# Attention and ELU on one core: first q and k turned half by half, conversion steps spread over the first group's units

## The chip, the cores and the metric

The kernel runs on one core of one Trainium2 chip. The metric is the device time of one execution in microseconds (us), lower is better. Names of engines: PE is TensorE, DVE is VectorE, ACT is ScalarE, POOL is GpSimd, SP is SyncE, which issues most of the DMAs here. PEld is PE's weight load.

## The reference

Routed attention first, then a two-layer product with an ELU between:

```python
batch, n_heads, seq, head_dim = (4, 8, 768, 64); n_clusters = 16
q_assign = np.argmax(np.einsum('bhsd,hcd->bhsc', q_n, c_n), axis=-1)   # q_n, k_n, c_n: unit rows
k_assign = np.argmax(np.einsum('bhsd,hcd->bhsc', k_n, c_n), axis=-1)
mask = q_assign[:, :, :, None] == k_assign[:, :, None, :]
scores = np.where(mask, 0.125 * np.matmul(q, k.transpose(0, 1, 3, 2)), -1e9)
attn_out = np.matmul(softmax(scores), v)
x = attn_out.transpose(0, 2, 1, 3).reshape(3072, 512)
h = x @ w_in                                        # 512 x 2048
g = np.where(h > 0.0, h, np.exp(np.minimum(h, 0.0)) - 1.0)
return (g @ w_out).astype(np.float32)               # 2048 x 512
```

The two weights come as 8-byte floats. The kernel reads them as pairs of 32-bit words and puts float32 weights together itself.

## The kernel before

**Slots.** Attention goes through 32 blocks n = (batch b, half of the queries, pair of heads pr); eight blocks make a batch. `slot(n)` computes the scores of block n, while the value product of block n-1 and the division of block n-2 run beside it. On PE a slot is: `row_sums` (L550) of n-2, `values` (L532) of n-1, sometimes `clusters_q` or `clusters_k` (L423), then six times a `plain` product (L494) and a `masked` one (L507) into one of three two-bank tiles of a ring. ACT turns each into exponentials (L516). DVE adds them (`sums_begin` L519, `sums_end` L524 and L525), divides (`divide` L564, L565; its last product L568 is on POOL), and transposes the next batch's k and q blocks (L634, L641, L645). "Slot n begins" below means where PE's first L532 of that slot stands in the trace.

**Clusters.** For each half, L423 compares q or k with the centroids; the told chain on DVE (L436, L438, L439, L449) finds the best cluster and transposes the marks; two ACT copies (L452) bring them to the other half of the partitions; for q, `mask_q` (L459, two operations on POOL) makes the mask that `masked` needs. The ACT copies and what follows wait in a list `later` until `flush()` is called.

**Start.** q and k of the first batch are loaded row by row and turned on PE: `turned_by_pe` (L573) is a product with the identity. One two-bank tile takes two pairs of q (one bank each, copied out by L584 on ACT and L586 on DVE), or both halves of one pair of k (L596). After all of k is turned, both halves' clusters are computed; the first three `plain` products stand ahead of telling them. q's second half and the batches after come in blocks that DVE transposes: `load_q` issues 16 DMAs, `load_k` 4, `load_v` 1, all on SP, all in the order of the program.

**Conversion.** Both weights come in 16 pieces of 1 MB (8 of w_in, 8 of w_out). `ask` (L296) loads a piece's words into a free place (`places`: words_w, parts of w_out's own space, and `spare`, each good up to some piece). A piece then takes four steps: `begin` (L316 and L324 on DVE, with an activation L326 on ACT put in `later`), and three times `join` (L336, L340, L346 on DVE); the second join frees the place, which may ask for the next piece. Four `weight_sum` steps (L371 to L377, DVE) follow. `weigh(n)` hands out steps by credit: each slot adds ROOM[n] to at most 2.5 that is left, and a begin costs 1.4, a join 1.25, a sum 2.2; no join follows a begin in the same slot, and a begin waits until its piece was asked for two slots earlier.

**First group's units.** The rows of x go in six groups of 512. The first product of a group takes four units of seven block products (L726), by a scheme of partial sums: PE writes one bank, ACT copies it into the next as the start of another sum (L766, L778), other copies go aside (L770, L786), DVE adds them in (L779, L788). `elu_exp` is an exponential on ACT (L736) and a clip on POOL (L737); `elu` (L740) and a difference (L805) are on DVE. The last part of a unit is put in `behind` and runs after the first product of the next one. `w_step` (L705, L707, L709 on POOL, each with a DMA L710) prepares the next unit's weights, `x_sum_step` (L682 to L688) the sums of x. `unit` calls `fill()` at four places. In the first group it does nothing before the change; there `weigh(32 + u)` hands out steps after each unit. The second product (L910) of the group comes next.

Of the kernel before, what the change touches and what calls it, by code (L numbers as in the profile page):

```python
# [61 lines left out]
def main_path(ctx, tc, c, q, k, v, centroids, moe_w_in, moe_w_out, out):  # L62
# [121 lines left out]
    def rows_of(t, src):  # L184
# [14 lines left out]
    first_k = [  # L199
        rows_of(t, k[0, 2 * pr : 2 * pr + 2]) for pr, t in enumerate(raw_k + kT[1][2:])  # L200
    ]
    load_v(0)
    load_q(0, 1)

# [62 lines left out]
    ]  # L267
    words, asked_in, now = {}, {}, -2
    asked, split, joined = 0, 0, 0
# [97 lines left out]
    def weight_sum(n):  # L367
# [12 lines left out]
    ROOM = (  # L380
        [2.3, 2.6, 3.0, 3.0, 1.4, 1.7, 2.6, 2.6] * (B - 1)
        + [2.3, 2.6, 4.0, 4.0, 3.0, 3.0, 3.0, 3.0]
        + [4.0, 5.0, 5.0, 5.0]
    )
# [12 lines left out]
    def weigh(n):  # L397
        nonlocal credit, now
        now = n
        credit = min(credit, 2.5) + ROOM[n]  # L400
        begun = False
        while steps and credit >= COST[steps[0][0]]:
            kind, m = steps[0]
            if kind == "join" and begun or kind == "sum" and n < len(blocks) + 2:
                return
            if kind == "begin" and asked_in.get(m, n) > n - 2 and n < len(blocks):
                return
            credit -= COST[kind]
            begun = begun or kind == "begin"
            weigh_step(*steps.pop(0))  # L410
# [165 lines left out]

    for two in range(2):
        ps = ring()
        for e in range(2):
            pr = 2 * two + e  # L580
            for t in range(HT):
                turned_by_pe(ps[:, e, ts(t, P)], first_q[pr], t)
            if e == 0:
                nc.scalar.copy(qT[0][pr], ps[:, e, :HS])  # L584
            else:
                nc.vector.tensor_copy(qT[0][pr], ps[:, e, :HS])  # L586
    nc.tensor.transpose(o_bank[:, :P], work[:, : 2 * D], ident)
    nc.vector.tensor_copy(cT, o_bank[:, :P])
    clusters_q(0, 0, d_bank)()
    flush()  # L590
    for pr in range(NPR):
        ps = ring()
        for t in range(NT):
            turned_by_pe(ps[:, t // HT, ts(t % HT, P)], first_k[pr], t)
        copy = nc.vector.tensor_copy if pr % 2 else nc.scalar.copy
        copy(kT[0][pr].rearrange("p (h s) -> p h s", h=2), ps[:, :, :HS])  # L596
    told = [clusters_k(0, half, ps) for half, ps in ((0, o_bank), (1, d_bank))]
    begun = [ring() for _ in range(3)]
    for kt in range(3):
        plain(0, kt, begun[kt])  # L600
    told[0]()
    flush()
    told[1]()
    ask()


    def slot(n):
# [41 lines left out]
        if n == 0:  # L649
            for kt in range(NT):  # L650
                s = begun[kt] if kt < 3 else ring()
                if kt >= 3:
                    plain(n, kt, s)
                masked(n, kt, s)
                exponential(kt, s)
                if kt == 2:
                    flush()
                elif kt == 3:
                    sums_begin()
            flush()  # L660
            return
        for kt in range(NT):
# [15 lines left out]
    def x_sum_step(k_, n):  # L678
        x11, x12, x21, x22 = x_parts(k_)
        t1, t2, t4 = x_s  # L680
        if n == 0:
            nc.gpsimd.tensor_tensor(t1, x12, x11, op=Alu.subtract)  # L682
        elif n == 1:
            nc.gpsimd.tensor_tensor(t2, x22, t1, op=Alu.subtract)
        elif n == 2:
            nc.gpsimd.tensor_tensor(x12, x22, x12, op=Alu.subtract)
        else:
            nc.gpsimd.tensor_tensor(t4, x21, t2, op=Alu.subtract)  # L688

# [430 lines left out]
    last_n = len(blocks) - 1  # L1120
    for n in range(len(blocks)):
        slot(n)
# [12 lines left out]
    values(last_n)  # L1135
    sums_end()
    take_sums(last_n - 1)
    divide(last_n - 1)
# [308 lines left out]
```

## Time and profile before

| what | us |
|---|---|
| median of three runs (lowest, highest) | 922.06 (921.91, 922.33) |
| the profiled execution | 922.52 |
| its span, first to last instruction | 920.7 |
| start, to the first L532 | 28.49 |
| slots 1 to 31 | 312.30 |
| last value product and the first group's units, to the first L910 | 60.33 |
| the rest | 519.58 |

The span leaves out about 1.8 us around the instructions. A profile row says: start and length in us, engine, line, operation, what it writes and reads, shapes, how many instructions were merged, and in brackets the idle time of its engine before it with what ended that wait. One float32 product of the program is two MATMUL rows. "SPq" is SP issuing a DMA. Groups read: busy time, mean ns of one, then idle time before them and its causes. A row by stretch ends with the granted clock of PE, the busy share of the DMA engines and GB/s.

### The profile page before, as it was taken

How to read it: one execution, taken by the hardware profiler on the slowest of the kernel's cores; microseconds unless marked ns; L12 is line 12 of the kernel's file. 1: busy time of each engine (PE TensorE's matmuls, PEld its weight loads, DVE VectorE, ACT ScalarE, POOL GpSimd, SP SyncE). 2: the span in 40 equal slices, each digit the busy share in tenths (PEclk: the TensorE clock that was granted, in tenths of full speed). 3: DMA queues.
4: the chain of work that ended last, by engine and by line, in shares of the span. 5: the costliest groups of instructions: out<-in, count | busy, mean ns of one | idle time of the engine just before them, and what ended most of it. 6: DMA issues, size and time to landing. Idle time of an engine off the chain costs nothing.

```text
span 920.7 us, 15833 instructions
## 1 busy us (share of the span) xinstructions
PE 900.6 (98%) x6080; PEld 686.5 (75%) x6083; DVE 672.9 (73%) x980; ACT 412.1 (45%) x811; POOL 207.4 (23%) x201
## 2 busy tenths in 40 slices
PE   7999999999999998999999999999999999999996
PEld 5444444444444447899988998999899989998996
DVE  4899999999999995772289953595359535953574
ACT  2777687777777773320133223322332233223321
POOL 1112020231303463850024102310231023102200
PEclk9999999999999999999999999999999999999999
DMA  6774564354425221110198762176217621762172
GB/s 166 220 189 88 135 155 87 127 101 90 115 82 141 94 86 69 68 47 1 58 288 307 257 198 60 46 255 195 66 46 255 198 64 45 252 203 64 44 224 81
DMA packets 143331, 121.22 MB, mean 132 GB/s; under 512 B 88208, under 2 KB 104592, under 8 KB 142224
## 3 DMA queue, kind: packets, MB, share of 16 engines
q1 hardware_dynamic: 142000, 115.93, 42.9%
q0 software_dynamic: 1248, 4.20, 1.5%
q8 instruction: 50, 0.82, 0.4%
q14 instruction: 33, 0.27, 0.1%
HBM read 100.96 MB, written 18.09 MB: 129 GB/s over the span
## 4 chain that ended last, share of the span: by engine, by line
PE 77%; DVE 15%; issue 3%; POOL 2%; ACT 1%; SPq 1%; DMA 1%; DVEq 0%; POOLq 0%; ACTq 0%
PE bank L910 22%; PE bank L726 21%; PE o_bank L532 8%; PE banks L494 8%; PE o_bank L910 4%; PE o_bank L726 4%; PE d_bank L910 2%; DVE sums_w L524 2%; DVE sums_w L519 2%; PE banks L507 2%; PE d_bank L726 2%; PE d_bank L550 2%; DVE sums_w L525 1%; POOL kq_g L737 1%; PE banks L573 1%
## 5 line engine op out<-in xcount | busy, mean ns | idle before, releaser
L516 ACT ACTIVATE p_out<-banks 128x768 f32<-128x768 f32 x192 | 154.3, 811 | 25.2 <-PE banks L507 21.2
L737 POOL TENSOR_SCALAR kq_g<-kq_g 128x512 f32<-128x512 f32 x96 | 71.4, 753 | 397.9 <-ACT kq_g L736 397.5
L532 PE MATMUL o_bank<-p_out,kq_g 128*64 128x384 f32 x768 | 129.3, 486 | 0.0
L532 PEld LDWEIGHTS o_bank<-p_out,kq_g 128*64 128x64 f32 x768 | 55.1, 137 | 68.8 <-issue 63.4
L740 DVE SCALAR_TENSOR_TENSOR kq_g<-kq_g,bank 128x512 f32<-128x512 f32 x72 | 48.2, 683 | 72.2 <-POOL kq_g L737 72.2
L726 PE MATMUL bank<-xT,w_in 128*128 128x256 f32 x384 | 90.7, 379 | 0.1
L568 POOL TENSOR_TENSOR xT<-xT,sums_w 128x384 f32<-128x384 f32 x32 | 35.9, 1120 | 203.4 <-DVE sums_w L565 176.1
L726 PEld LDWEIGHTS bank<-xT,w_in 128*128 128x128 f32 x384 | 72.6, 190 | 10.1
L726 PE MATMUL bank<-xT,spare 128*128 128x256 f32 x288 | 67.7, 386 | 3.6 <-ACT bank L778 3.6
L726 PE MATMUL bank<-x_sum,w_in 128*128 128x256 f32 x288 | 68.0, 379 | 0.0
L726 PEld LDWEIGHTS bank<-xT,spare 128*128 128x128 f32 x288 | 55.7, 194 | 11.7 <-POOL kq_g L737 4.0
L524 DVE TENSOR_TENSOR sums_w<-sums_w,p_out 128x1536 f32<-128x1536 f32 x32 | 61.4, 1918 | 3.3
L910 PE MATMUL bank<-w_out,kq_g 128*128 128x128 f32 x512 | 62.9, 275 | 0.0
L910 PEld LDWEIGHTS bank<-w_out,kq_g 128*128 128x128 f32 x512 | 60.4, 192 | 0.3
L519 DVE TENSOR_TENSOR sums_w<-p_out 128x1536 f32<-128x1536 f32 x32 | 58.9, 1842 | 2.0 <-ACT p_out L516 2.0
L726 PEld LDWEIGHTS bank<-x_sum,w_in 128*128 128x128 f32 x288 | 54.6, 190 | 7.3
L736 ACT ACTIVATE kq_g<-bank 128x512 f32<-128x512 f32 x72 | 41.9, 598 | 39.3 <-PE bank L726 39.1
L970 DVE TENSOR_TENSOR kq_g<-kq_g 128x1024 f32<-128x1024 f32 x36 | 43.7, 1221 | 5.3 <-PE bank L910 5.3
L459 POOL TENSOR_SCALAR kq_g<-w_out,big,minus 128x768 bf16<-128x768 bf16 x16 | 32.7, 2052 | 59.1 <-ACT w_out L452 59.1
L494 PE MATMUL banks<-kq_g 64*128 64x384 f32 x192 | 39.7, 492 | 0.7 <-ACT p_out L516 0.7
L494 PE MATMUL banks<-x_sum,xT 64*128 64x384 f32 x192 | 39.6, 493 | 0.6 <-ACT p_out L516 0.6
L494 PE MATMUL banks<-kq_g,xT 64*128 64x384 f32 x192 | 39.6, 491 | 0.0
(233 smaller groups left out, 1707.5 us busy)
## 6 DMA issues: line engine op xcount, KB each, us to landing
spare<-w_far SPq DMA_DIRECT2D x60, 256.0 KB, 2.7
kq_g<-in_v_dram SPq DMA_DIRECT2D x32, 384.0 KB, 3.6
sums_w<-far_s_s SPq DMA_DIRECT2D x40, 256.0 KB, 4.0
words_w<-far_s_s SPq DMA_DIRECT2D x29, 256.0 KB, 3.4
words_w<-in_moe_w_out_dram SPq DMA_DIRECT2D x6, 1024.0 KB, 5.0
out_dram<-p_out SPq DMA_DIRECT2D x24, 256.0 KB, 2.6
w_out<-in_q_dram SPq DMA_DIRECT2D x112, 48.0 KB, 2.4
words_w<-far_a_s SPq DMA_DIRECT2D x21, 256.0 KB, 3.5
```

Of the source, the lines that this page charges most:

```text
L494: nc.tensor.matmul(s[:, e, :HS], lhsT=kT[b % 2][pr][rows, ts(kt, P)], rhs=qT[half][pr][rows], start=True, stop=False,)
L516: nc.scalar.activation(probs[kt], s[:, :, :HS], Act.Exp, scale=SCALE)
L519: nc.vector.tensor_tensor(add_to, probs_all[:, : 4 * HS], probs_all[:, 4 * HS : 8 * HS], op=Alu.add)
L524: nc.vector.tensor_tensor(add_to, add_to, probs_all[:, 8 * HS :], op=Alu.add)
L532: nc.tensor.matmul(o_bank[64 * e : 64 * e + 64, :HS], lhsT=v_raw[n % 2][:, e, kt], rhs=probs[kt][:, e], start=(kt == 0), stop=(kt == NT - 1),)
L568: nc.gpsimd.tensor_tensor(x_of(n), x_of(n), r_of, op=Alu.mult)
L726: nc.tensor.matmul(bank[:, ts(f, QS)], lhsT=left[:, ch, ts(f, P)], rhs=right[:, ch], start=first and f == 0 and ch == 0, stop=ch == 1, ski ...
L736: nc.scalar.activation(to, bank.rearrange("p (f n) -> p f n", f=2), Act.Exp)
L737: nc.gpsimd.tensor_scalar(to, to, 1.0, 0.0, op0=Alu.min, op1=Alu.max)
L740: nc.vector.scalar_tensor_tensor(to, to, -1.0, bank.rearrange("p (f n) -> p f n", f=2), op0=Alu.add, op1=Alu.max)
L910: nc.tensor.matmul(bank[:, :P], lhsT=left[:, f], rhs=right[:, f], start=first and f == 0, stop=last and f == 3, skip_group_check=True,)
L970: nc.vector.tensor_tensor(b[to][:, f], b[x][:, f], b[y][:, f], op=op)
```

## The change

First loads: the third and fourth pair of k now go where q's second half is to come, v of block 1 is loaded at once, and q's second half later. q and k are turned one half of one pair at a time, each into one bank, six banks in turn, and copied by ACT alone; clusters of k's first half are told while the second half is turned. Block 0's scores follow in a part of their own, `slot_first`, with no conversion step. q's second half is transposed in slot 2 and told in slot 3. ROOM is smaller in the first batch and at the end of the last. The last place for words, p_out, is added after the last value product. All steps that are left run one by one in the four `fill` places of the first group's units. The first group's sums of x go from POOL to DVE.

```diff
     first_k = [
-        rows_of(t, k[0, 2 * pr : 2 * pr + 2]) for pr, t in enumerate(raw_k + kT[1][2:])
+        rows_of(t, k[0, 2 * pr : 2 * pr + 2])
+        for pr, t in enumerate(raw_k + [raw_q_all[:, :S], raw_q_all[:, S:]])
     ]
     load_v(0)
-    load_q(0, 1)
+    load_v(1)
...
-    words, asked_in, now = {}, {}, -2
+    words, asked_in, now = {}, {}, 0
...
     ROOM = (
-        [2.3, 2.6, 3.0, 3.0, 1.4, 1.7, 2.6, 2.6] * (B - 1)
-        + [2.3, 2.6, 4.0, 4.0, 3.0, 3.0, 3.0, 3.0]
-        + [4.0, 5.0, 5.0, 5.0]
+        [0.0, 1.0, 1.3, 1.4, 1.4, 1.7, 2.6, 2.6]
+        + [2.3, 2.6, 3.0, 3.0, 1.4, 1.7, 2.6, 2.6] * (B - 2)
+        + [2.3, 2.6, 4.0, 4.0, 2.6, 2.6, 2.6, 2.6]
     )
...
-            if kind == "join" and begun or kind == "sum" and n < len(blocks) + 2:
+            if kind == "join" and begun or kind == "sum":
                 return
-            if kind == "begin" and asked_in.get(m, n) > n - 2 and n < len(blocks):
+            if kind == "begin" and asked_in.get(m, n) > n - 2:
                 return
...
-    for two in range(2):
-        ps = ring()
-        for e in range(2):
-            pr = 2 * two + e
-            for t in range(HT):
-                turned_by_pe(ps[:, e, ts(t, P)], first_q[pr], t)
-            if e == 0:
-                nc.scalar.copy(qT[0][pr], ps[:, e, :HS])
-            else:
-                nc.vector.tensor_copy(qT[0][pr], ps[:, e, :HS])
-    nc.tensor.transpose(o_bank[:, :P], work[:, : 2 * D], ident)
-    nc.vector.tensor_copy(cT, o_bank[:, :P])
-    clusters_q(0, 0, d_bank)()
-    flush()
-    for pr in range(NPR):
-        ps = ring()
-        for t in range(NT):
-            turned_by_pe(ps[:, t // HT, ts(t % HT, P)], first_k[pr], t)
-        copy = nc.vector.tensor_copy if pr % 2 else nc.scalar.copy
-        copy(kT[0][pr].rearrange("p (h s) -> p h s", h=2), ps[:, :, :HS])
-    told = [clusters_k(0, half, ps) for half, ps in ((0, o_bank), (1, d_bank))]
-    begun = [ring() for _ in range(3)]
-    for kt in range(3):
-        plain(0, kt, begun[kt])
-    told[0]()
-    flush()
-    told[1]()
-    ask()
+    def turn(to, t, n):
+
+        for i in range(HT):
+            turned_by_pe(to[:, ts(i, P)], t, n + i)
+
+    turns = 0
+
+    def turned(to, t, n):
+
+        nonlocal turns
+        bank = pair_tiles[turns % 3][:, turns // 3 % 2]
+        turns += 1
+        turn(bank, t, n)
+        nc.scalar.copy(to, bank[:, :HS])
+
+    def slot_first():
+
+        for pr in range(NPR):
+            turned(qT[0][pr], first_q[pr], 0)
+        nc.tensor.transpose(o_bank[:, :P], work[:, : 2 * D], ident)
+        nc.vector.tensor_copy(cT, o_bank[:, :P])
+        clusters_q(0, 0, d_bank)()
+        for pr in range(NPR):
+            turned(kT[0][pr][:, :HS], first_k[pr], 0)
+        told = [clusters_k(0, 0, o_bank)]
+        flush()
+        for pr in range(NPR):
+            turned(kT[0][pr][:, HS:], first_k[pr], HT)
+        told.append(clusters_k(0, 1, d_bank))
+        told[0]()
+        flush()
+        told[1]()
+        load_k(1, 0)
+        ask()
+        load_q(0, 1)
+        load_k(1, 1)
+        for kt in range(NT):
+            s = ring()
+            plain(0, kt, s)
+            masked(0, kt, s)
+            exponential(kt, s)
+            if kt == 2:
+                flush()
+            elif kt == 3:
+                sums_begin()
...
-        if at == 1:
+        if at == (1 if b else 3):
             told = clusters_q(b, 1, d_bank)
...
-        if at == 0:
+        if at == 0 and b:
             nc.vector.transpose(qT_all[1], raw_q_all)
-            if more:
-                load_k(b + 1, 0)
-                load_k(b + 1, 1)
-        elif at == 1 and more:
+        if at == 1 and b and more:
             load_q(b + 1, 0)
+        if at == 0 and more:
+            load_k(b + 1, 0)
+            load_k(b + 1, 1)
         elif 2 <= at < 6 and more:
             nc.vector.transpose(kT[(b + 1) % 2][at - 2], raw_k[at % 2])
+            if n == 2:
+                nc.vector.transpose(qT_all[1], raw_q_all)
+                load_q(1, 0)
             if at < 4:
                 load_k(b + 1, at)
...
     def x_sum_step(k_, n):
...
+        by = nc.gpsimd if k_ else nc.vector
         if n == 0:
-            nc.gpsimd.tensor_tensor(t1, x12, x11, op=Alu.subtract)
+            by.tensor_tensor(t1, x12, x11, op=Alu.subtract)
...
-    for n in range(len(blocks)):
+    slot_first()
+    for n in range(1, len(blocks)):
         slot(n)
...
     sums_end()
+    for n in range(2):
+        places.append((p_out[:, ts(n, 2048)].unsqueeze(1), len(pieces)))
+    ask()
     take_sums(last_n - 1)
...
+    def fill_weights():
+        flush()
+        if steps:
+            weigh_step(*steps.pop(0))
+
...
-        run(unit(0, u, finish_attention if u == 0 else None))
-        weigh(len(blocks) + u)
+        run(unit(0, u, finish_attention if u == 0 else None, fill_weights))
```

More of the change, by code (lines that the diff above doesn't have):

```diff
@@ L647, in slot @@
         weigh(n)
[L649 to L661, printed above, removed]
         for kt in range(NT):
@@ L680, in x_sum_step @@
         t1, t2, t4 = x_s
+        by = nc.gpsimd if k_ else nc.vector
         if n == 0:
-            nc.gpsimd.tensor_tensor(t1, x12, x11, op=Alu.subtract)
+            by.tensor_tensor(t1, x12, x11, op=Alu.subtract)
         elif n == 1:
-            nc.gpsimd.tensor_tensor(t2, x22, t1, op=Alu.subtract)
+            by.tensor_tensor(t2, x22, t1, op=Alu.subtract)
         elif n == 2:
-            nc.gpsimd.tensor_tensor(x12, x22, x12, op=Alu.subtract)
+            by.tensor_tensor(x12, x22, x12, op=Alu.subtract)
         else:
-            nc.gpsimd.tensor_tensor(t4, x21, t2, op=Alu.subtract)
+            by.tensor_tensor(t4, x21, t2, op=Alu.subtract)
     def w_parts(u):
```

## The prediction

> **What bounds the kernel now.** I read the page, then busy time by stretch (start, attention slots, first group's units, the rest), then who waited on TensorE inside the slots, then the timeline where PE pauses.
>
> ```profile
> span 920.7 us, 15833 instructions
> PE 900.6 (98%) x6080; PEld 686.5 (75%) x6083; DVE 672.9 (73%) x980; ACT 412.1 (45%) x811; POOL 207.4 (23%) x201
> 0.00:28.49 28.49, 20.77 (x205) 13.65 (x206) 16.00 (x41) 10.75 (x17) 2.69 (x9) 1.00 0.73 210
> 28.49:340.79 312.30, 311.56 (x2091) 144.86 (x2091) 300.97 (x336) 234.92 (x380) 83.75 (x56) 1.00 0.47 119
> 340.79:401.12 60.33, 56.27 (x258) 45.85 (x257) 43.58 (x54) 23.09 (x43) 35.82 (x36) 0.97 0.20 69
> PE banks L494 <- ACT p_out L516: 0.7, 1, 0.7
> ```
>
> Columns after the stretch's length: PE, PEld, DVE, ACT, POOL busy, clock, DMA. PE bounds nearly everything: between the first and the last value product it pauses once, for 0.7 us. So moving DVE work is worth nothing by itself; a change can only win where PE really waits: in the first 28.5 us, at that one pause, and in the first group's units. The start and the units, from the timeline:
>
> ```profile
> 5.96 2.83 PE L573 MATMUL banks<-ident,p_out 128*64 128x128 f32 x24 [0.57 <-ACT x_sum L584]
> 9.36 1.51 PE L573 MATMUL banks<-ident,p_out 128*64 128x128 f32 x12 [0.58 <-ACT x_sum L584]
> 16.92 1.53 PE L573 MATMUL banks<-ident,kq_g 128*64 128x128 f32 x24 [0.18 <-ACT xT L596]
> 26.61 0.33 PE L507 MATMUL banks<-kq_g,w_out 64*128 64x384 bf16 x1 [0.87 <-ACT w_out L452]
> 40.47 3.65 POOL L459 TENSOR_SCALAR kq_g<-w_out,big,minus 128x768 bf16<-128x768 bf16 x2 [22.24 <-ACT w_out L452]
> ...
> 358.58 1.63 DVE L340 SCALAR_TENSOR_TENSOR w_out<-words_w,w_out 128x1024 f32<-128x1024 uint32 x1
> 360.24 0.37 SPq L296 DMA_DIRECT2D words_w<-in_moe_w_out_dram  x1
> 365.30 0.69 DVE L316 TENSOR_SCALAR w_out<-words_w 128x1024 uint32<-128x1024 uint32 x1 [3.53 <-DMA words_w<-in_moe_w_out_dram]
> 366.63 1.15 ACT L326 ACTIVATE sums_w<-sums_w,off 128x1024 uint32<-128x1024 uint32 x1 [5.42 <-DVE sums_w L324]
> 368.62 0.60 ACT L778 COPY bank<-o_bank 128x512 f32<-128x512 f32 x1
> 369.37 3.52 PE L726 MATMUL bank<-xT,spare 128*128 128x256 f32 x8 [3.58 <-ACT bank L778]
> 369.37:372.73 3.36, 3.36 (x9) 2.71 (x10) 0.95 (x2) 0.37 (x1) 2.74 (x4) 0.53 0.20 78
> ```
>
> The last piece of w_out reuses words_w, free only after L340; its words land 5 us later, DVE stands on them, the L326 activation stands on DVE, L778 stands behind L326 in ACT's queue, and PE stands on L778. Then PE runs at a granted clock of 0.53. In the first rows, PE waits for ACT's copy of one bank before it fills the other bank of the same tile.
>
> **Start: first q and k by halves.** Durations from these rows: a turn of a half is 12 rows, 1.28 us at the early pace (12 rows in 1.51 at 9.36), 0.65 later (24 in 1.53 at 16.92); an ACT copy of 128x384 0.48 (L584); L423 of one half 0.85; a told chain L436 to L449 2.4 on DVE; a pair of L452 copies 1.04; an exponential about 0.75. Consecutive turns now go to different tiles, so both 0.57 waits go. Four q turns: 3.84 + 4 x 1.28 = 8.96, last copy 9.73 (now 11.55). Centroids' copy and L423: assignment of q begins about 11.3 (now 12.72), half of L423 at the slow pace. k half 0: turns 11.2 to 13.8, ACT copy to 14.4, L423 to 15.3. Half 1: turns 15.3 to 17.9, copy 18.5, L423 19.4, while DVE tells half 0 (15.35 to 17.7) and POOL masks q. The L452 pair for half 0 queues behind ACT's k copies: 18.5 to 19.6. Scores follow: exponentials 20.3 to 22.5, L452 pair of half 1 to 23.55, masked products of kt 3 at 23.6, and two more pairs of 0.81 + 0.17: the value product starts at 25.5 instead of 28.49. **3.0 us.**
>
> The rule I weigh here: the Trainium skill, TensorE: Matmul & The Clock Gate, Part 1 (The HAM clock gate), says one busy window of about 3.4 us gives the full clock, the window running free. Here PE starts at 3.84, with gaps of 0.57, and the pace doubles only after the 9.36 row. With the gaps gone the rule would grant at about 7.3: the fourth turn and L423 speed up, and everything follows about 1 us sooner, limited at k's fourth tile (landed 12.1): 4.0. I take the row, 3.0.
>
> What SP is moved past: q's half 1 (16 DMAs, 0.66 each, from 6.2) now goes behind k(1,0), which must wait until half 1 of its buffer is turned (about 16), and behind three 1 MB pieces. SP: k 16 to 18.6, pieces to 20.1, 16 q plus k(1,1) 13.2 us more, plus holds on a full queue (3.1 and 5.9 us on two k DMAs now): v(2) issued at 39 to 41, landed 3.9 later, 43 to 45; slot 3 needs it at 25.5 + 2 x 9.71 = 44.9. I take no stall; bound -1.2. v(1), now early, costs nothing: v(0) comes first. The 1.74 transpose L634 moves to slot 2, where DVE has room because ROOM drops from 3.0 to 1.3. Behind it SP now sends q(1,0) (16 DMAs, 10.6 us) and k(1,2) from about 43, a slot later than today: landed near 56 and 58.7, wanted by L645 and L641 in slot 4 from about 59.5; no cost, and DVE can lag some us there before PE feels it. L423 of q's half 1 moves from slot 1 to 3: -0.78, +0.78.
>
> **Slot 4's mask.** q half 1 is now told in slot 3 and used in slot 4. The POOL row at 40.47 began 1.44 us after its slot's value product and took 3.65, with DVE's sums beside it: 5.1. PE reaches the masked product at 3.97 + 0.65 = 4.65. **-0.45**; zero if only the first of the two masks is waited for. I take the wait, since the start's rows show waits drawn for a whole tile.
>
> **Slots 1 to 31.** Walking the credit rule: before, 57 of 68 steps run in the slots; after, 53. Slot 28 now has 2.5 + 3.0 - 3 x 1.25 = 1.75, enough for a fourth step; after, 1.35 is not. The pause at 318.04 follows from just that slot (DVE from 306.8 to 315.2 on L336, L340, L346, L316, L324), stretched by POOL's x_sum operations beside it. These move to DVE, four of 0.6 to 0.7 in slots 27 to 30, where 2.6 replaces 3.0; DVE's own 5.7 a slot (L519, L524, L525, L564, L565), three joins (3.45) and 0.6 make 9.75 of 9.71 in slot 28, but with one begin 7.6 in 27 and 29. Slot 29 took 10.72 instead of 9.71. **+1.0**, bound 0.3. Other slots stay PE's (9.71, or 10.49 with clusters): today L436 leaves its bank at worst 0.6 us before PE wants it (slot 22), and DVE has no more to do than today. Cost zero while that cover lasts, up to 0.5 if not.
>
> **Units.** The last piece now goes to p_out, asked for when value product 31 is done (345), landed by about 351, begun about 375: no wait. So the pause 3.58 goes, the slow-clock cost goes (eight rows 3.36 against 1.73: 1.63), and the 0.37 at 397.43 behind the weight sums goes: 5.58. Fifteen steps (11 at 1.15 to 1.6, 4 sums at 2.3 to 2.6) go one to a place, four places a unit. DVE per unit: 4 L740, L779, L788, L805 at 0.7 = 4.9, plus 4 x 1.35 = 10.3 of 12.1; today it idles 9 us there:
>
> ```profile
> L740 DVE SCALAR_TENSOR_TENSOR kq_g<-kq_g,bank 128x512 f32<-128x512 f32 x11 | 7.3, 680 | 9.0 <-POOL kq_g L737 9.0
> L737 POOL TENSOR_SCALAR kq_g<-kq_g 128x512 f32<-128x512 f32 x16 | 17.5, 1106 | 12.1 <-ACT kq_g L736 11.8
> ```
>
> Inside a unit PE needs from DVE only L779: ready 6.0 us after the unit's start (L778's end), wanted at 8.6, so 1.9 spare. Ahead of it stand three L740, L805 and one step, done at about 7. The fourth unit has four sums and overruns by about 4.5, into the second product, which wants the last c21 only 8 us in. The rule against this: the Trainium skill, SBUF — State Buffer, "SBUF: two separate sides": a DVE operation with two SBUF inputs and a GpSimd operation exclude each other for the whole instruction. L737 shows it (1106 mean here; 630 alone). By the rule each of four clips a unit lets DVE idle 0.63 after a step: 12.8 of 12.1, about 0.7 for three units, 2.1 lost. By the row, clips already ran under L336 and L340 (358.37, two in 2.31) without PE pausing, and the spare 1.9 takes it. I take 0.3. **+5.3**, bounds 3.5 and 5.6.
>
> **Sum.** 3.0 - 0.45 + 1.0 + 5.3 = 8.85. The profiled execution took 922.52 (span 920.7 and 1.8 around it), 0.46 above the median 922.06: 913.67 in its terms, **913.2** against the median.
>
> **Rivals.**
> A (0.2): the start gives little, because SP's queue brings q half 1 or v(2) late, or ACT, now the only copier, lags. For: holds of 3.1 and 5.9 on SP. Against: 4 us between landing and need today. 0.5 - 0.45 + 1.0 + 5.3 = 6.35: 915.7.
> B (0.11): the lock between DVE and POOL eats half of the units' gain: 3.0 - 0.45 + 1.0 + 2.3 = 5.85: 916.2. For: L709 at 387 to 394 stood behind three clips of 6.84 in all while sums ran.
> C (0.04): single banks do not free PE (turns still wait for copies): the start is no sooner: 3.0 less, 916.2. Against: the waits stand only inside a tile.
> D (0.03), slower: clips ahead of L779 are each held to 2.64 (as the longest of the three in 387 to 394, beside a weight sum) in units 1 to 3: 3 x 2.0 - 1.9 = 4.1 a unit, 12.3 in all, against 8.85: 925.5. It decides from 1.6 us a clip. Against: only sums are that long, and they stand in the last unit alone.
> Forecast 0.62.
>
> **Numbers.** The forecast's own range is 911 to 915; A, B and C reach 916.2; the early clock gives 912.2, and with no mask wait 911.7. Range 911.0 to 916.3. No change means within 0.2% (1.8 us), about what this kernel's measurement can tell. Faster takes nearly all of the forecast, A, B, C: 0.95; same 0.03, where two of them meet; slower 0.02, most of D.
>
> **What would show it.** Right: the first L532 at 25 to 26; no PE pause and no 0.5 clock between 340 and 400; no L316 waiting for a DMA in the units; slot 29 at 9.71; L459 ending after PE reaches slot 4's masked product. Wrong: L532 waiting for v, L634 for q, L726 for L779, or a second product that starts later than 48.4 + 2 us after value product 31.

## The result, and the profile after

The median of four runs of the changed kernel is 915.62 us (915.41 to 915.98), beside 922.19 (921.91 to 922.84) of the kernel before: a ratio of 0.9928, 95% interval 0.9911 to 0.9945. The gain is real and 6.6 us. 913.2 was predicted; 915.62 lies inside the stated range of 911.0 to 916.3, but above the forecast's own 911 to 915. The profiled executions took 915.41 and 922.52, and their spans differ by 7.13. That is the sum that has to be accounted for.

In the changed file most lines have moved by one to nine: L532 is now L533 (value product), L494 and L507 are L495 and L508 (scores and mask), L573 is L574 (turn), L316, L324 and L326 are L317, L325 and L327 (a begin), L726 is L735 (block product), L779 is L788, L805 is L814, L910 is L919; L705 and L709 are L714 and L718 (POOL's `w_step`), L740 is L749 (`elu`).

The page, and busy time by stretch (start, slots, last value product and units; columns as before):

```profile
span 913.5 us, 15842 instructions
PE 898.5 (98%) x6083; PEld 685.4 (75%) x6083; DVE 673.8 (74%) x980; ACT 416.9 (46%) x819; POOL 201.5 (22%) x197
...
0.00:24.68 24.68, 19.79 (x205) 13.73 (x205) 11.04 (x35) 15.39 (x26) 3.08 (x9) 1.00 0.71 217
24.68:337.41 312.73, 311.58 (x2090) 144.85 (x2090) 297.93 (x338) 233.89 (x378) 74.14 (x52) 1.00 0.48 121
337.41:393.90 56.49, 55.06 (x260) 44.65 (x257) 47.78 (x57) 24.12 (x44) 33.66 (x34) 1.00 0.20 72
```

Read the first number of each row against the row of before: the start is 3.81 shorter, the slots are 0.43 longer, the units' stretch is shorter and its granted clock is 1.00 where it had 0.97. PE stays busy for 98% of the span, so it still bounds the kernel. Where PE pauses, from its timeline; first the start:

```profile
3.87 4.99 PE L574 MATMUL banks<-ident,p_out 128*64 128x128 f32 x48 [3.87 <-DMA p_out<-in_q_dram]
8.79 0.33 PE L597 MATMUL o_bank<-ident,spare 128*128 128x128 f32 x1
9.50 0.85 PE L424 MATMUL d_bank<-x_sum,cT 128*32 128x384 f32 x8 [0.38 <-DVE cT L598]
10.29 2.84 PE L574 MATMUL banks<-ident,w_out 128*64 128x128 f32 x48
13.06 1.48 PE L424 MATMUL o_bank<-xT,cT 128*32 128x384 f32 x8
...
22.81 0.33 PE L508 MATMUL banks<-kq_g,w_out 64*128 64x384 bf16 x1 [0.64 <-ACT w_out L453]
```

All four turns of q are one row of 48 with no pause in it; so are the four of a half of k. In before, the same work was broken twice by 0.57. The comparison of q (L424) starts at 9.50 instead of 11.81.

In the slots three things changed, besides the comparison of q's second half, which moved from slot 1 to slot 3. Slot 29 went from 10.72 to 9.71. Slot 3's value product waited 0.30 for v of block 2, so that slot 2 took 10.18 instead of 9.71 (0.47 more), and slot 23 grew from 10.49 to 11.42:

```profile
39.72 1.11 SPq L179 DMA_DIRECT2D kq_g<-in_v_dram  x2
...
44.63 1.83 PE L533 MATMUL o_bank<-p_out,kq_g 128*64 128x384 f32 x10 [0.30 <-DMA kq_g<-in_v_dram]
...
247.94 1.18 DVE L347 SCALAR_TENSOR_TENSOR w_out<-w_out,sums_w 128x1024 f32<-128x1024 f32 x1
...
249.64 0.69 DVE L325 TENSOR_SCALAR sums_w<-words_w 128x1024 uint32<-128x1024 uint32 x1
250.36 1.15 ACT L327 ACTIVATE sums_w<-sums_w,off 128x1024 uint32<-128x1024 uint32 x1 [1.28 <-DVE sums_w L325]
251.42 0.47 ACT L560 ACTIVATE sums_w<-d_bank 128x384 f32<-128x384 f32 x1
251.79 0.48 ACT L561 ACTIVATE sums_w<-d_bank 128x384 f32<-128x384 f32 x1
252.41 0.85 PE L424 MATMUL d_bank<-kq_g,cT 128*32 128x384 f32 x8 [0.86 <-ACT sums_w L561]
```

In slot 23 a begin stands behind a third join (L347) on DVE. Its activation L327 is ahead of `take_sums` (L560, L561) in ACT's queue and waits 1.28 us for DVE; L561 is what frees d_bank, and PE's L424 wants that bank. The smaller ROOM of the first batch had shifted which step falls where; in before, slot 22's begin had no third join ahead of it, and e1 below, which keeps the first batch's ROOM of before, has 10.49 for slot 23.

In the units the long pause and the slow clock are gone, and two new pauses of 0.66 stand on DVE's L788. The timeline of the second unit:

```profile
359.02 1.29 POOL L718 TENSOR_TENSOR spare<-w_in,spare 128x512 f32<-128x512 f32 x1
359.05 1.81 DVE L814 TENSOR_TENSOR kq_g<-kq_g 128x512 f32<-128x512 f32 x1
...
360.78 0.68 DVE L317 TENSOR_SCALAR w_out<-words_w 128x1024 uint32<-128x1024 uint32 x1
361.38 2.06 DVE L325 TENSOR_SCALAR sums_w<-words_w 128x1024 uint32<-128x1024 uint32 x1
361.61 1.28 POOL L714 TENSOR_TENSOR spare<-w_in 128x512 f32<-128x512 f32 x1
...
363.37 0.67 DVE L749 SCALAR_TENSOR_TENSOR kq_g<-kq_g,bank 128x512 f32<-128x512 f32 x1
...
363.97 0.68 DVE L788 TENSOR_TENSOR o_bank<-o_bank,spare 128x512 f32<-128x512 f32 x1
...
364.80 1.53 PE L735 MATMUL o_bank<-xT,spare 128*128 128x256 f32 x6 [0.66 <-DVE o_bank L788]
```

L814 takes 1.81 where it takes 0.69 with POOL at rest, and L325 2.06 instead of 0.69. Each ends 0.55 after the end of a POOL TENSOR_TENSOR (L718 at 360.31, L714 at 362.89) and nearly covers it: as if it had been held until POOL was done. The step ahead of L788 thus costs 2.7 instead of 1.35, L814 1.1 more, and L788 comes too late. The third unit has the same (0.66), the fourth 0.11.

The account of the 7.13: start +3.81, slot 3's wait -0.47, slot 23 -0.93, slot 29 +1.01, units (first L726 or L735 to first L910 or L919: 55.76 to 51.92) +3.84, all else -0.13.

### The profile page after: what moved, and what is told of

Its sections match the earlier page's. It is cut to its first block, busy times and chain, and to the rows that moved or that the text cites. A ratio compares the mean times of both kernels' runs of the same rounds, so it can differ in the third digit from the quotient of the medians.

```text
span 913.5 us, 15842 instructions
## 1 busy us (share of the span) xinstructions
PE 898.5 (98%) x6083; PEld 685.4 (75%) x6083; DVE 673.8 (74%) x980; ACT 416.9 (46%) x819; POOL 201.5 (22%) x197
## 4 chain that ended last, share of the span: by engine, by line
PE 88%; DVE 7%; POOL 2%; issue 1%; DMA 1%; ACT 1%; DVEq 0%; SPq 0%; POOLq 0%; ACTq 0%
PE bank L919 23%; PE bank L735 22%; PE banks L495 12%; PE o_bank L533 11%; PE o_bank L735 4%; PE o_bank L919 4%; PE banks L508 3%; PE d_bank L551 2%; PE d_bank L919 2%; PE d_bank L735 2%; PE d_bank L424 1%; PE banks L574 1%; DVE sums_w L525 1%; DVE sums_w L520 1%; DVE sums_w L526 1%
## 5 line engine op out<-in xcount | busy, mean ns | idle before, releaser
L533 PE MATMUL o_bank<-p_out,kq_g 128*64 128x384 f32 x768 | 129.4, 486 | 0.3 <-DMA kq_g<-in_v_dram 0.3
L533 PEld LDWEIGHTS o_bank<-p_out,kq_g 128*64 128x64 f32 x768 | 55.0, 137 | 69.4 <-issue 62.7
L749 DVE SCALAR_TENSOR_TENSOR kq_g<-kq_g,bank 128x512 f32<-128x512 f32 x72 | 48.3, 684 | 67.0 <-POOL kq_g L746 67.0
L735 PE MATMUL bank<-xT,w_in 128*128 128x256 f32 x384 | 90.7, 379 | 0.0
L735 PEld LDWEIGHTS bank<-xT,w_in 128*128 128x128 f32 x384 | 72.6, 190 | 10.1
L735 PE MATMUL bank<-x_sum,w_in 128*128 128x256 f32 x288 | 68.0, 379 | 0.0
L735 PE MATMUL bank<-xT,spare 128*128 128x256 f32 x288 | 66.3, 379 | 0.7 <-DVE bank L788 0.7
L919 PE MATMUL bank<-w_out,kq_g 128*128 128x128 f32 x512 | 62.9, 275 | 0.0
L520 DVE TENSOR_TENSOR sums_w<-p_out 128x1536 f32<-128x1536 f32 x32 | 57.1, 1785 | 7.6 <-ACT p_out L517 7.6
L525 DVE TENSOR_TENSOR sums_w<-sums_w,p_out 128x1536 f32<-128x1536 f32 x32 | 59.0, 1845 | 3.3 <-DVE sums_w L520 0.5
L735 PEld LDWEIGHTS bank<-xT,spare 128*128 128x128 f32 x288 | 54.6, 190 | 8.4 <-issue 1.0
L919 PEld LDWEIGHTS bank<-w_out,kq_g 128*128 128x128 f32 x512 | 60.4, 192 | 0.3
L735 PEld LDWEIGHTS bank<-x_sum,w_in 128*128 128x128 f32 x288 | 54.6, 190 | 7.3
L495 PE MATMUL banks<-x_sum,xT 64*128 64x384 f32 x192 | 39.8, 492 | 0.0
L495 PE MATMUL banks<-kq_g,xT 64*128 64x384 f32 x192 | 39.6, 491 | 0.0
L495 PE MATMUL banks<-kq_g 64*128 64x384 f32 x192 | 39.6, 491 | 0.0
```

Source lines behind the costliest of these rows:

```text
L495: nc.tensor.matmul(s[:, e, :HS], lhsT=kT[b % 2][pr][rows, ts(kt, P)], rhs=qT[half][pr][rows], start=True, stop=False,)
L520: nc.vector.tensor_tensor(add_to, probs_all[:, : 4 * HS], probs_all[:, 4 * HS : 8 * HS], op=Alu.add)
L525: nc.vector.tensor_tensor(add_to, add_to, probs_all[:, 8 * HS :], op=Alu.add)
L533: nc.tensor.matmul(o_bank[64 * e : 64 * e + 64, :HS], lhsT=v_raw[n % 2][:, e, kt], rhs=probs[kt][:, e], start=(kt == 0), stop=(kt == NT - 1),)
L735: nc.tensor.matmul(bank[:, ts(f, QS)], lhsT=left[:, ch, ts(f, P)], rhs=right[:, ch], start=first and f == 0 and ch == 0, stop=ch == 1, ski ...
L749: nc.vector.scalar_tensor_tensor(to, to, -1.0, bank.rearrange("p (f n) -> p f n", f=2), op0=Alu.add, op1=Alu.max)
```

## Experiments

Every kernel was timed beside the kernel before, whose median was 922.19 to 923.17, and the ratio is to that. "v0" is the first value product, "slots" runs from it to value product 31, "units" as in the account.

| kernel | median us | ratio to before, 95% interval | v0 | slots | units |
|---|---|---|---|---|---|
| before | 922.19 | | 28.49 | 312.30 | 55.76 |
| after | 915.62 | 0.9928 (0.9911 to 0.9945) | 24.68 | 312.73 | 51.92 |
| e1_units_only | 919.91 | 0.9973 (0.9964 to 0.9982) | 27.98 | 311.28 | 53.30 |
| e2_place_behind | 913.91 | 0.9915 (0.9898 to 0.9931) | 24.45 | 312.31 | 50.48 |
| e3_wstep_late | 913.65 | 0.9909 (0.9893 to 0.9926) | 24.99 | 312.29 | 50.44 |
| e4_flush_late | 914.32 | 0.9919 (0.9902 to 0.9935) | 24.79 | 311.28 | 51.90 |
| e5_same_tile | 919.65 | 0.9969 (0.9956 to 0.9981) | 28.70 | 312.31 | 51.90 |
| e6_told_late | 915.58 | 0.9926 (0.9909 to 0.9942) | 25.17 | 312.27 | 51.85 |
| e7_room_3 | 917.64 | 0.9948 (0.9932 to 0.9965) | 25.09 | 312.53 | 53.92 |
| e8_xsum_pool | 916.30 | 0.9934 (0.9917 to 0.9951) | 24.29 | 313.62 | 51.90 |
| e9_lump | 918.21 | 0.9950 (0.9934 to 0.9967) | 25.16 | 312.27 | 54.58 |
| e10_no_p_out | 914.87 | 0.9913 (0.9896 to 0.9929) | 24.36 | 312.28 | 52.10 |
| e11_three_mends | 912.72 | 0.9892 (0.9875 to 0.9908) | 25.03 | 311.28 | 50.50 |
| e12_four_mends | 914.74 | 0.9910 (0.9893 to 0.9926) | 25.17 | 311.28 | 50.99 |

The intervals of neighbours overlap, so the readings below rest on the stretches of one profile each. Where nothing was touched the units agree within 0.1 us (51.85 to 51.92 in after, e4, e5, e6, e8); v0 does not, it varies from 24.29 to 25.17. The wait for v of block 2 is in the profile of after alone: slot 2 takes 9.71 in the others.

**e1: the units' part alone, on the kernel before.**

```diff
+        by = nc.gpsimd if k_ else nc.vector          # x sums of the first group
...
+    for n in range(2):
+        places.append((p_out[:, ts(n, 2048)].unsqueeze(1), len(pieces)))
+    ask()
...
-        run(unit(0, u, finish_attention if u == 0 else None))
-        weigh(len(blocks) + u)
+        run(unit(0, u, finish_attention if u == 0 else None, fill_weights))
```

ROOM 2.6 in the last four slots and `fill_weights` come with it; the start and the first batch stay as before.

> The kernel before with the units' part alone (fill places, p_out as a place for words, 2.6 in the last four slots, the first group's x sums on DVE); start, load order and the first batch's ROOM stay as before. Theory 1 (the parts add up; each removes its own wait of PE): first L532 at 28.5, slot 29 at 9.71 instead of 10.72, first group's units 51.9 instead of 55.8, so a span of 920.7 - 1.0 - 3.8 = 915.9. Rival (the parts need each other: without the lighter first batch the slots or the units get new pauses): span 917.5 or more.

The span fell by 4.01: slots 1.02, units 2.46, and 0.51 of the start, which was not touched (its full clock was granted at 9.74 instead of 10.72). Slot 29 took 9.71, as theory 1 has it, but not its 51.9 for the units: neither forecast holds as it stands. The units are 1.4 longer than in the changed kernel although fewer steps (12 instead of 15) are left, since a third join (2.81) and a weight sum (2.28) now fall in the place ahead of L779 and hold PE 0.99 and 2.06. So it is the kind of step in that place that decides, not the number of steps.

**e2: the place ahead of L788 put behind it.**

```diff
         nc.vector.tensor_tensor(b2, b2, m5, op=Alu.add)
+        if k_ == 0 and u:
+            fill()
         fill()
...
-            fill()
+            if k_:
+                fill()
             elu(c21, b3)
```

> After, with the fill place that stands ahead of L788 (in the unit's last part) moved to just behind L788, where two steps now run. Theory 1 (PE's new pauses of 0.66, 0.66 and 0.11 come only from what stands ahead of L788 on DVE): no pause of PE on L788, first group's units 50.2 instead of 51.9, span 911.8. Rival (DVE has too much to do in a unit, so a moved step only moves the pause): units 51.5 or more.

The second unit in its timeline:

```profile
358.39 1.79 DVE L816 TENSOR_TENSOR kq_g<-kq_g 128x512 f32<-128x512 f32 x1
...
360.73 0.70 DVE L788 TENSOR_TENSOR o_bank<-o_bank,spare 128x512 f32<-128x512 f32 x1
361.33 1.05 DVE L317 TENSOR_SCALAR w_out<-words_w 128x1024 uint32<-128x1024 uint32 x1
...
363.32 1.89 PE L735 MATMUL o_bank<-xT,spare 128*128 128x256 f32 x8
```

The difference (here L816) is as long as before, but L788 is now done 1.9 us before PE wants its bank. The units take 50.48, 1.44 less, and no pause on L788 is left; one of 0.21 on an ACT copy is new.

**e3: POOL's L714 issued one place later**, so that it does not run beside the step.

```diff
         fill()
-        if u < 3:
+        if u < 3 and k_:
             w_step(k_, u + 1, 0)
...
         nc.vector.tensor_tensor(b4, b4, u3, op=Alu.add)
+        if u < 3 and k_ == 0:
+            w_step(k_, u + 1, 0)
```

> After, with the first weight sum of the next unit on POOL (L714 with its DMA) issued behind the second fill place instead of the first, in the first group only; all steps on DVE stay where they are. Theory 1a (POOL's operation beside the begin step holds DVE up: L325 took 2.06 instead of 0.69): L325 back at 0.7, L788 about 1.3 sooner, both pauses of 0.66 gone, units 50.2 to 50.5, span 911.9. Theory 1b (it is the number of operations ahead of L788, POOL has no part in it): pauses stay, units 51.9, span 913.5.

```profile
358.08 0.69 DVE L816 TENSOR_TENSOR kq_g<-kq_g 128x512 f32<-128x512 f32 x1
...
358.69 1.10 DVE L317 TENSOR_SCALAR w_out<-words_w 128x1024 uint32<-128x1024 uint32 x1
...
359.21 1.73 POOL L718 TENSOR_TENSOR spare<-w_in,spare 128x512 f32<-128x512 f32 x1
359.71 1.78 DVE L325 TENSOR_SCALAR sums_w<-words_w 128x1024 uint32<-128x1024 uint32 x1
...
362.01 0.69 DVE L788 TENSOR_TENSOR o_bank<-o_bank,spare 128x512 f32<-128x512 f32 x1
```

The begin stands ahead of L788 as in the changed kernel, yet both 0.66 pauses are gone: with one POOL operation less beside them, the difference takes 0.69 and L788 comes at 362.01 instead of 363.97. One detail of theory 1a missed: L325 was to be back at 0.7 and still takes 1.78, since L718 now runs beside it. One pause of 0.43 remains in the fourth unit, behind a weight sum. e2 and e3 are two ways to the same 1.4: a step ahead of L788, together with two POOL operations beside what stands there, is the cause.

**e4: slot 22's `flush` put behind slot 23's `take_sums`.**

```diff
             take_sums(n - 2)
+        if n == 23:
+            flush()
...
-        flush()
+        if n != 22:
+            flush()
```

> After, with what slot 22 put off for ACT (two L453 copies and the begin's activation L327) issued behind slot 23's three operations on the row sums (L560 to L562) instead of ahead of them; DVE's work and order are the same. Theory 1 (PE's pause of 0.86 in slot 23 comes from ACT's queue: L327 waits for a late begin on DVE, L560 stands behind it, and L424 wants the bank that L561 reads): slot 23 at 10.49 instead of 11.42, span 912.6. Rival (DVE is simply late in slots 22 and 23): slot 23 at 11.2 or more, or the pause turns up in slot 24.

Slot 23 is back at 10.49, the slots take 311.28 in all, and the units are as they were: L327's place in ACT's queue was the whole of it.

**e5: two turns in succession into one tile.**

```diff
-        bank = pair_tiles[turns % 3][:, turns // 3 % 2]
+        bank = pair_tiles[turns // 2 % 3][:, turns % 2]
```

> The changed kernel with one edit: two turns in succession go to the two banks of one tile, as before the change, instead of to two tiles; everything else of the changed start stays. Theory 1 (single banks of different tiles give most of the start's gain): each second turn waits for ACT's copy of the first, 0.57 us for each of two tiles of q and four of k, about 3.4 us in all, and the first value product goes from 24.7 back to about 28. Theory 2 (the gain is from telling the first half's clusters while the second half is turned, and from the clock's earlier grant): only the two waits in q come, at the slow pace, and the first value product starts at 25.3 to 25.9. The slots and the units are the same in both.

PE's timeline:

```profile
5.90 2.29 PE L574 MATMUL banks<-ident,p_out 128*64 128x128 f32 x24 [0.57 <-ACT x_sum L591]
8.78 0.88 PE L574 MATMUL banks<-ident,p_out 128*64 128x128 f32 x12 [0.58 <-ACT x_sum L591]
10.30 0.85 PE L424 MATMUL d_bank<-x_sum,cT 128*32 128x384 f32 x8 [0.39 <-DVE cT L598]
11.08 0.88 PE L574 MATMUL banks<-ident,w_out 128*64 128x128 f32 x12
12.53 1.53 PE L574 MATMUL banks<-ident,w_out 128*64 128x128 f32 x24 [0.58 <-ACT xT L591]
```

All six waits come (two in q, four in k), and v0 is 28.70: the whole gain of the start is gone by one index, although clusters are still told half by half. The granted clock rose at 7.50 here, earlier than in the profile of after (8.32), so it isn't the clock. But e5 is not the start of before: that had the two waits in q and one of 0.18 in k, and e5's other waits in k come of turning k by halves in its order of banks. So e5 shows that the new start needs the order of banks, not that the order alone is worth 3.8.

**e6: half 0's clusters compared and told only after half 1 is turned.**

```diff
-        told = [clusters_k(0, 0, o_bank)]
         flush()
         for pr in range(NPR):
             turned(kT[0][pr][:, HS:], first_k[pr], HT)
+        told = [clusters_k(0, 0, o_bank)]
```

> The changed kernel with one edit: the clusters of k's first half are compared and told only after the second half has been turned. Theory 1 (turns in single banks are most of the start's gain): the told chain of half 0 starts about 2.4 us later, ACT's copies and the first masked product about 0.95 later (20.35 instead of 19.43), masked of kt 3 the same, and the first value product is at about 25.6 instead of 24.7. Theory 2 (telling one half while the other is turned is most of it): the first value product is at 27 or later.

From q's L424 to v0 the changed kernel takes 15.18 us, and so do eight of the other profiles with its telling, whatever the clock had done before; e2 takes 15.48, since its first turns of k take 3.15 instead of 2.84. e6 takes 15.60: the overlap of telling and turning is worth 0.42, less than half of the 0.95 expected, since PE, with L424 moved, reached the scores 1.2 us sooner. By its median e6 is not to be told from the changed kernel.

**e7 and e8: what ended the pause in slot 29.** e7 has ROOM 3.0 again in the last four slots, with the sums of x on DVE; e8 has the sums of x on POOL again, with ROOM 2.6.

```diff
-        + [2.3, 2.6, 4.0, 4.0, 2.6, 2.6, 2.6, 2.6]
+        + [2.3, 2.6, 4.0, 4.0, 3.0, 3.0, 3.0, 3.0]     # e7
...
-        by = nc.gpsimd if k_ else nc.vector
+        by = nc.gpsimd                                  # e8
```

> The changed kernel with one edit: ROOM is 3.0 again for the last four slots of attention; the first group's sums of x stay on DVE. By the rule of credit slot 28 then takes three joins and a begin again, slot 30 two joins and a begin, slot 31 three joins, and four steps fewer are left for the units. Theory 1 (the pause in slot 29 came of the fourth step): DVE has 5.7 + 3.45 + 1.4 and 0.65 of x sums, 11.2 us in a slot of 9.71, and slot 29 takes 10.7 to 11.2. Theory 2 (it came of POOL's sums of x, which stretched DVE's steps): all slots from 28 on take 9.71. The units have 11 steps to do instead of 15, and the step ahead of L788 differs; theory 1 of the units (a long or a stretched step in the place ahead of L788) puts pauses only where a begin, or the sums, stands in that place.

> The changed kernel with one edit: the first group's sums of x go back to POOL; ROOM stays at 2.6. Theory 1 (ROOM ended slot 29's pause): slots 28 to 31 take 9.71 each and the time is that of the changed kernel within 0.3 us. Theory 2 (POOL's sums beside DVE's joins made it): one of the slots 28 to 31 takes 10.2 to 10.8, and the time is 0.5 to 1.0 longer.

In e7 slot 28 takes three joins and a begin as in before, and yet slots 28 to 30 took 9.71; only slot 31 was longer, by 0.29. In e8, with the sums on POOL and no fourth step in slot 28, slot 29 took 9.71 too, but slot 31 took 11.06, 1.35 more. There three joins stand beside the last sum of x, and `sums_begin` (L520) behind them, stretched as well, holds ACT and then PE:

```profile
328.69 2.18 DVE L347 SCALAR_TENSOR_TENSOR w_out<-w_out,sums_w 128x1024 f32<-128x1024 f32 x1
...
330.80 2.83 DVE L520 TENSOR_TENSOR sums_w<-p_out 128x1536 f32<-128x1536 f32 x1
...
334.59 0.92 PE L495 MATMUL banks<-kq_g 64*128 64x384 f32 x4 [1.08 <-ACT p_out L517]
```

So slot 29's pause needed both, the fourth step and the sums on POOL: either one alone left that slot at 9.71. By what each put back elsewhere, the sums on POOL are the dearer of the two. How POOL does it is seen in before, in slot 28 and, for the pause, in slot 29:

```profile
307.00 1.85 POOL L568 TENSOR_TENSOR xT<-xT,sums_w 128x384 f32<-128x384 f32 x1 [5.75 <-DVE sums_w L565]
...
307.91 2.02 DVE L340 SCALAR_TENSOR_TENSOR w_out<-w_out 128x1024 f32<-128x1024 uint32 x1
...
308.81 2.27 POOL L684 TENSOR_TENSOR x_sum<-xT,x_sum 128x512 f32<-128x512 f32 x1
...
309.96 2.19 DVE L346 SCALAR_TENSOR_TENSOR w_out<-w_out,sums_w 128x1024 f32<-128x1024 f32 x1
...
311.03 2.29 POOL L705 TENSOR_TENSOR spare<-w_in 128x512 f32<-128x512 f32 x1
...
312.08 1.78 DVE L316 TENSOR_SCALAR w_out<-words_w 128x1024 uint32<-128x1024 uint32 x1
...
318.04 0.92 PE L494 MATMUL banks<-kq_g 64*128 64x384 f32 x4 [0.74 <-ACT p_out L516]
```

L568 ends at 308.85, L340 1.08 later, L684 1.15 after that, L346 1.07 later, L705 1.17 later, L316 0.54 later: each ends about its own working time after the other engine's one, so the two take turns (L340 takes 1.22 beside an idle POOL, L316 0.68). A sum of x on POOL thus costs DVE about 1.1 us; on DVE itself it costs 0.68. e7's units take 53.92, the longest but for e9, with pauses of 1.21 and 2.17 on L788, although three steps fewer are left: as in e1, the steps that fall ahead of L788 are others.

**e9: p_out kept, nothing spread; four steps in a lump after each unit.**

```diff
-        run(unit(0, u, finish_attention if u == 0 else None, fill_weights))
+        run(unit(0, u, finish_attention if u == 0 else None))
+        for _ in range(4):
+            if steps:
+                weigh_step(*steps.pop(0))
```

> The changed kernel with one edit: nothing is handed out at the four places inside the first group's units; after each unit four steps follow in a lump, as the kernel before did it, and p_out stays as the last place for words. Theory 1 (the free place ended the long wait; spreading the steps is what puts pauses on L788): no wait for words, no pause of 0.66 at the second and third unit, the stretch of the units 50.3 to 51.2 instead of 51.9. Theory 2 (spreading the steps is needed): four steps of 1.2 to 2.6 in a row stand ahead of the next unit's L749 and L788 and hold PE 1 to 3 us in at least two units, stretch 53 or more.

**e10: p_out left out, steps spread.**

```diff
-    for n in range(2):
-        places.append((p_out[:, ts(n, 2048)].unsqueeze(1), len(pieces)))
-    ask()
```

> The changed kernel with one edit: p_out isn't a place for words; the last piece goes to words_w when the second join of the piece before has freed it, as before the change; the steps stay spread. Theory 1 (spreading alone covers the load: three places, some 9 us, lie between that join and the last piece's begin, and the words landed 5 us after being asked for): no wait of L317 for words, the stretch of the units 51.9 and the time as the changed kernel's within 0.3 us. Theory 2 (p_out is what ended the wait): L317 waits 1 to 3.5 us for its words, PE stands behind it, the granted clock falls again, and the stretch is 53 to 57.

e9 is theory 2: PE waits 1.78 and 2.35. The first is a begin's activation again (L327, 373.75 to 374.90, behind L325), in ACT's queue ahead of the copy L787, which began at 375.75; the second is a sum ahead of L788:

```profile
376.49 3.69 PE L735 MATMUL bank<-xT,spare 128*128 128x256 f32 x16 [1.78 <-ACT bank L787]
392.90 1.97 PE L735 MATMUL o_bank<-xT,spare 128*128 128x256 f32 x8 [2.35 <-DVE o_bank L788]
```

No word is waited for in e9, so the free place did its part, but without the spreading the lumps give most of it back. In e10 the wait for words is only 0.44:

```profile
373.49 1.76 DVE L317 TENSOR_SCALAR w_out<-words_w 128x1024 uint32<-128x1024 uint32 x1 [0.44 <-DMA words_w<-in_moe_w_out_dram]
```

It makes one pause on L788 0.86 instead of 0.66 and the units 52.10 instead of 51.92. That is near theory 1, which had no wait at all: spreading alone brought nearly all of the units' gain; p_out added 0.2.

**e11: e2 and e4 together, and v of block 2 loaded ahead of k's second part. e12: the same with e3.**

```diff
         load_q(0, 1)
-        load_k(1, 1)
...
+        if n == 1:
+            load_k(1, 1)
```

> The changed kernel with three edits together: v of block 2 is loaded ahead of k's second part in slot 1; slot 22's flush comes behind slot 23's sums; and in the units the place for a step stands behind L788 instead of ahead of it. By the single runs: slot 2 at 9.71 (-0.3 to -0.5), slot 23 at 10.49 (-0.93), units 50.5 instead of 51.9 (-1.4): about 2.7 less than the changed kernel, a span of 910.5 to 911.2 and a time of 912.4 to 913.2. Rival: two of these gains are the same time seen twice, and the time is 913.5 or more.

> The same three edits, and POOL's L714 for the next unit is issued behind the first group's third place, away from the DVE steps. If its lock on DVE still costs something there, the last pause (0.21) goes and the span is 0.1 to 0.3 below the kernel with three; otherwise the two are the same within 0.2.

e11 has the slots of e4 and the units of e2: these gains add. What the third edit is worth is not shown: slot 2 takes 9.71 with it, as in the profiles of the others without it. Its median of 912.72 is the lowest of all; the interval of its ratio ends where that of the changed kernel begins. e12 was to be equal or better and is 2.0 slower. POOL's operations, moved back, now stand beside the third unit's difference (1.30 instead of 0.73 in e11), so the begin behind it comes 0.63 later, and with it its activation, which stands ahead of the copy L801 in ACT's queue; PE waits for that copy:

```profile
375.78 1.15 ACT L327 ACTIVATE sums_w<-sums_w,off 128x1024 uint32<-128x1024 uint32 x1 [3.31 <-DVE sums_w L325]
...
377.31 0.58 ACT L801 COPY spare<-bank 128x512 f32<-128x512 f32 x1
...
377.94 1.35 PE L739 MATMUL bank<-x_sum,w_in 128*128 128x256 f32 x5 [0.95 <-ACT spare L801]
```

In e11 the activation starts at 375.15 and the copy holds PE 0.21. e12 loses another 0.87 in the second product, where PE waits for an L753 (L749 of the changed kernel) that starts at 400.85 instead of 399.09. The clips ahead of it are not longer (the last takes 2.65 in both), they only start 1.75 later. As far as these profiles tell, POOL's work was moved from one tight place to another.

## Why the prediction was right, and where its terms were off

The way was forecast rightly, and each of the three places where PE was to gain did gain. The total is 1.72 short of the 8.85 in spans because errors of both signs met: the start gave 0.81 more and the mask's 0.45 was not lost, while the units gave 1.46 less, and slot 23 (0.93), slot 2 (0.47) and the rest (0.13) had been taken as 0. That 1.26 of these 2.99 was made up elsewhere is luck.

- **Start, +3.0; measured +3.81.** That the turns gain only in different tiles is shown by e5. The term after q's comparison was right: 1.50 us (16.68 from L423 to v0 before, 15.18 after) beside the 1.6 of the prediction; e6 shows 0.42 of it to be the overlap of telling and turning, and how the rest is made up was not tested. The first step was mis-sized: q's L423 was to come about 1.4 sooner and came 2.31 sooner, because the slow pace was taken from the row for all four turns. In this profile the rule that was weighed and set aside did better than the row: the clock was granted at 8.32 and the sum by the rule was 4.0. But it isn't that the gaps kept the clock down: in e5, with both gaps of 0.57, it rose at 7.50. Nor does an earlier grant bring all that the rule promised: in e6 and e10 (7.36 and 6.63) the fourth turn then waits 0.35 and 0.18 for its own load. The ten profiles with this start and the telling unchanged have v0 between 24.29 and 25.17, mean 24.80; the two with the old start have 27.98 and 28.49. By these means the start is worth 3.4, between row and rule.
- **v of block 2, bound -1.2, taken as 0; measured -0.47** in this profile. Issued at 39.72 and landed just before 44.63, inside the forecast of 39 to 41 and 43 to 45; but v0 was 24.68 and not 25.5, so it was wanted at 44.2 and not 44.9. The step had no reserve here; in the other profiles it held. This is the one part of rival A that came; that A's 915.7 lies so near the measured 915.62 is chance, since A's start gave less and the measured one more.
- **Slot 4's mask, -0.45; measured 0.** Both of POOL's mask operations end at 56.55 + 3.86 = 60.41, and PE starts its first masked product at 59.89: so it does not wait for both. The prediction had named this case and chosen the other; the sign that it gave (L459 ends after PE reaches the masked product) came and cost nothing. (Its 3.97 + 0.65 is 4.62, not 4.65, which changes nothing.)
- **Slot 29, +1.0; measured +1.01.** Right in size and in mechanism: it named a fourth step in slot 28, stretched by POOL's sums of x, and e7 and e8 show that the pause needed both. The change takes away both at once, where either would have done for this slot.
- **Other slots, 0 to -0.5; measured -0.93** in slot 23. The prediction looked at DVE's distance from PE in such slots, not at a begin's activation in ACT's queue ahead of the sums that free d_bank.
- **Units, +5.3; measured +3.84.** The three removed costs (5.58) are gone in full: no long wait for words, no clock of 0.53, no wait of 0.37. The prediction gave the wait for words to p_out alone; e9 (p_out without spreading, no wait) and e10 (spreading without p_out, 0.44) show that either one ends all or most of it. The new loss was set at 0.3 and is 51.92 - (55.76 - 5.58) = 1.74, of which 1.43 are the three pauses. The step of this sum that was off is the choice between row and rule. By the rule of the Trainium skill (SBUF — State Buffer, "SBUF: two separate sides") the prediction would have had about 3.5 here, which is nearer; the row used in its place showed clips under joins, in a place where PE had time to spare. But it is not the clips that hold L788: it is POOL's `w_step` operations (L714, L718), which the prediction did not count, beside L814 and L325. This is rival B's mechanism, at 1.4 us more than was allowed; B's own figure was 3.0.
- **Clips of 2.64 ahead of L779 (D)** did not come: no pause in the units is over 0.66. Rival C is refuted by the row of 48 turns.
- **Signs of being wrong.** Two that the prediction listed came, both small: L533 waited 0.30 for v, and L735 waited 0.66 twice for L788. A third, a second product later than 48.4 + 2 after value product 31, was set too tight: 48.4 is four units of 12.1, while the forecast itself leaves 55.76 - 5.3 = 50.5 for the units.

## What to carry to other kernels

When steps of another job are spread into a pipelined loop, place each one behind the last instruction that PE waits for on that engine, not ahead of it, and put the dependent instruction that it leaves on another engine's queue behind that engine's own urgent work: in these kernels a begin cost PE nothing, 0.66, 0.93 or 1.78 us by where it stood and what ran beside it. Price such a step beside what the other engines will be doing at that moment, from a row where both run, and count all of the other engine's operations, not only the kind that a row happens to show. And turn or fill the buffers of a ring in the order that keeps neighbours in different tiles: one index was worth 4 us in e5.

## What the runs showed of the hardware

- DVE and POOL take turns even where the DVE operation has one tensor input: TENSOR_SCALAR L325 (uint32, 128x1024) takes 0.69 alone, 1.78 and 2.06 beside a POOL TENSOR_TENSOR; the two-input L814 takes 0.69 alone and 1.81. Each stretched operation ends nearly its own undisturbed time after the other engine's one. That clips on POOL under joins had cost PE nothing in before said nothing on this; PE merely had time there. A DVE operation that reads its second input from a bank that PE writes is not stretched: in the profile of after L749 took 0.69 at 353.85, wholly inside a POOL operation (L716, 353.77 to 355.05), and 0.67 at 363.37 with POOL at rest.
- PE's full clock was granted between 6.6 and 9.2 us in the twelve profiles with the new start, and at 9.74 and 10.72 in the two with the old one, while PE always began at 3.8 to 4.0. Early grants occurred with pauses of 0.57 in the work as well (7.50 in e5), so one profile's grant is a poor price for pauses at the start.
